# Attention into a snake MLP on one core: both token halves of two head pairs finished as one in the first stage

## The chip, the cores and the metric

The kernel runs on one core of a Trainium2 chip. The metric is the device time of one execution in microseconds (us). The kernel before took 214.25, 214.41 and 214.91 us in three runs, a median of 214.41 us. One execution was also recorded by the hardware profiler; every duration below comes from that record.

## The reference

Attention over chunks of 32 tokens, each chunk seeing 8 memory rows, itself, 16 tokens to the left and 8 to the right; then, per token, a feed-forward layer with the activation h + sin²(αh)/α.

```python
B, H, S, D = 4, 8, 768, 64              # batches, heads, tokens, head width
for c in range(S // 32):                # scores are scaled by 1/sqrt(D)
    k_full = concat([mem_k, k[:, :, l_start:r_end]])
    v_full = concat([mem_v, v[:, :, l_start:r_end]])
    a = softmax(scale * q_c @ k_full.T)
    out[:, :, chunk] = a @ v_full
x = out.transpose(0, 2, 1, 3).reshape(B * S, H * D)      # 3072 x 512
h = x @ w_in                                             # 512 x 2048
g = h + sin(alpha * h) ** 2 / alpha
return g @ w_out                                         # 2048 x 512
```

## The kernel before

**Tiling.** Tokens are taken in windows of 96 (three chunks), eight windows to a batch; a *half* is four windows, 384 tokens. Heads go in pairs (`hp`, 0 to 3). A window's keys lie in 128 columns of the transposed keys `kT`: 64 context keys, 8 memory keys, 56 more. Scores are computed keys by tokens, so that `exp` gives the tile `pt` (128 keys x 768: two heads of a pair by four windows of 96) which is at once the stationary operand of the product with the values `vw`. A 65th column of `vw` holds ones, so that each value product also gives the sum of the exponentials; `normed` (L352) takes the reciprocal of that column (L355, on VectorE) and multiplies (L356, VectorE, 96 x 512) into a block `x_blk`. Four transposes on TensorE (L368) and one copy (L371, 128 x 384) turn such a block into `xT`, the input of the feed-forward layer with the channels on the partitions.

**Stages.** Batch 0's attention is done alone, in a first stage; then four stages follow, each doing the feed-forward layer of one batch while the attention of the next is woven into it. In a stage the layer's first product (L426) makes tiles of 128 hidden channels by 768 tokens, a `sin` (L441, ScalarE), a square (L449 or L446) and L453 (VectorE) finish each, and the second product (L464) is fed in between. The first stage is the only one that this change touches.

**Order.** The order is written out by hand, as words that are carried out from left to right; each word issues its instructions to the engines, and every engine runs its own in that order, waiting for semaphores where data or buffers are not ready. The words that matter here, with `hp` and half as digits:

- `k2`, `l2`: transposes of the keys and queries of pair 2 (L276, 12 on TensorE); `K2V`, `L2V`: their copies to `kT` and `qT` (L287 or L301, last letter A for ScalarE, V for VectorE; after each `K` a small VectorE copy L293 of the ends)
- `a6V`: the cast of the third pair's queries to bf16 on VectorE (L655)
- `s01`: scores of pair 0, half 1 (`u_scores`: two mask products L319, eight score products L327, then `exp` L334 on ScalarE)
- `v01`: their value products and normalisation (`u_values`: eight products L346, then L355 and L356)
- `T01`, `t10`: transposes and copy into `xT`, on ScalarE (`T`) or VectorE (`t`)
- `z1`: a product of zeros (L688), 512 columns; it keeps TensorE at work
- `dm`, `I02`, `I27`: loads of the memory values and of `w_in` on GpSimd's queue (L667, L213); `Cs`: two fills of `kst` on GpSimd (L810, L811); `Ws`: loads the table for `sin` on ScalarE (L701)
- `V068`: the values of pairs 3 (heads 6 and 7) on GpSimd's queue (L172, L179)

PSUM has eight banks. `Banks` (L59) hands out a bank or an even pair of banks, the longest free first; scores, value products and a feed-forward tile take a pair, transposes one. `Slots` (L45) hands out six `x_blk` buffers in the same way. The kernel ends the first stage with `Ws`; the next stage begins with `b0 h0`, the first tile of L426 (four products for half 0, which need the half 0 of all four pairs in `xT`, then four for half 1).

## Time and profile before

| what | us |
|---|---|
| median of three runs | 214.41 (214.25 to 214.91) |
| the profiled execution, its own time | 215.01 |
| its span, first to last instruction | 213.2 |
| first L426 product starts (end of the first stage on TensorE) | 24.91 |
| TensorE clock granted | 1.0 throughout |

| group in the first stage, 12 to 25 us | count | mean us of one |
|---|---|---|
| L334 `exp`, ScalarE | 8 | 0.822 |
| L356 multiply 96 x 512, VectorE | 8 | 0.687 |
| L355 reciprocal 96 x 8, VectorE | 8 | 0.196 |
| L346 value products, 65 columns, TensorE | 64 | 0.195 |
| L371 copies into `xT`, ScalarE, 128 x 384 | 4 | 0.478 |
| L371 copies into `xT`, VectorE, 128 x 384 | 4 | 0.344 |
| L301 copies of 128 x 768, ScalarE | 2 | 0.830 |
| L701 load of the `sin` table, ScalarE | 1 | 1.283 |

How to read it: products on TensorE are pipelined, so that a group's length is set by the spacing of its starts and not by the sum of the durations. "Idle before" in a line is the time in which the engine did nothing ahead of the instruction, with what released it; "issue" there means that the engine waited for nothing that the profile shows.

### The profile page before, as it was taken

The page shows a single profiled execution, that of the slowest core. Times are in us where ns is not written, and L with a number is a line of the kernel's source. Part 1 is how long each engine was busy: PE and PEld are TensorE (multiplying, and loading weights), DVE is VectorE, ACT ScalarE, POOL GpSimd, SP SyncE. Part 2 cuts the span into 40 slices and gives each one's busy share as a digit, 9 for nine tenths or more (in the row PEclk, how much of TensorE's full clock was granted, in tenths as well). Part 3 has the DMA queues.
Part 4 walks back from the last instruction along what each step waited for, and adds up shares of the span by engine and source line. Part 5 has one row for each costly group of instructions (what it writes and reads, how often), then busy time and mean ns, then how long its engine had stood idle before and what let it go on. Part 6 is the DMA issues. An engine that isn't in the chain of part 4 may idle for free.

```text
span 213.2 us, 4484 instructions
## 1 busy us (share of the span) xinstructions
PE 203.4 (95%) x1716; PEld 114.9 (54%) x1736; DVE 140.0 (66%) x218; ACT 143.3 (67%) x229; POOL 99.9 (47%) x142
## 2 busy tenths in 40 slices
PE   7888899999999999999999999999999999999994
PEld 2366665565555556555455555554555565654453
DVE  4788788999542749975856649897257187865010
ACT  2588898976857469978846199887846189891110
POOL 8989505589596197109993038664000022200000
PEclk9999999999999999999999999999999999999999
DMA  5999999999999999999993259999944400000312
GB/s 153 311 169 141 209 207 204 205 149 184 126 170 155 163 122 137 146 112 171 144 215 95 71 124 126 170 128 126 134 101 108 135 3 0 2 3 0 148 49 98
DMA packets 95852, 27.80 MB, mean 130 GB/s; under 512 B 84808, under 2 KB 92376, under 8 KB 95832
## 3 DMA queue, kind: packets, MB, share of 16 engines
q0 software_dynamic: 69152, 13.64, 84.7%
q1 hardware_dynamic: 25720, 12.68, 28.3%
q10 hardware_dynamic: 960, 1.21, 1.7%
q8 instruction: 13, 0.21, 0.5%
q14 instruction: 7, 0.06, 0.1%
HBM read 29.66 MB, written 6.29 MB: 169 GB/s over the span
## 4 chain that ended last, share of the span: by engine, by line
PE 74%; DVE 9%; ACT 5%; DMA 5%; issue 4%; POOL 1%; DVEq 0%; ACTq 0%
PE ps L464 37%; PE ps L426 29%; DMA kq_f<-in_k_dram 4%; DVE gT L453 3%; PE ps L416 3%; DVE s L449 3%; PE ps L387 2%; ACT pt L334 2%; ACT u L441 2%; ACT s L446 2%; PE ps L368 1%; POOL s L449 1%; DMA memk_f<-in_mem_k_dram 1%; DVE kT L287 1%; DVE x_blk L356 1%
## 5 line engine op out<-in xcount | busy, mean ns | idle before, releaser
L464 PE MATMUL ps<-w_out_sb,gT 128*128 128x512 bf16 (+1 forms) x382 | 86.9, 370 | 1.3 <-issue 0.3
L426 PE MATMUL ps<-xT,w_in_sb 128*128 128x384 bf16 x512 | 85.9, 326 | 0.6 <-DVE gT L453 0.4
L453 DVE SCALAR_TENSOR_TENSOR gT<-s,inv_alpha,ps 128x768 bf16<-128x768 f32 x64 | 63.1, 1012 | 12.3 <-ACT s L446 5.2
L426 PEld LDWEIGHTS <-w_in_sb 128*128 128x128 bf16 x512 | 49.8, 98 | 35.1 <-issue 1.7
L441 ACT ACTIVATE u<-ps,alpha_sb 128x768 f32<-128x768 f32 x64 | 56.6, 894 | 16.9 <-PE ps L426 14.4
L464 PEld LDWEIGHTS <-gT 128*128 128x128 bf16 x400 | 37.1, 98 | 37.2 <-DVE gT L453 0.2
L449 POOL TENSOR_TENSOR s<-u 128x768 f32<-128x768 f32 x11 | 17.2, 1567 | 69.1 <-ACT u L441 57.0
L401 ACT ACTIVATE pt<-ps,biasm 128x256 bf16<-128x256 f32 x72 | 27.2, 488 | 10.5 <-PE ps L387 10.5
L471 DVE COPY o_sb<-ps 128x512 f32<-128x512 f32 (+1 forms) x15 | 10.0, 669 | 27.4 <-PE ps L464 25.5
L449 DVE TENSOR_TENSOR s<-u 128x768 f32<-128x768 f32 x23 | 21.9, 953 | 7.6 <-ACT u L441 7.5
L446 ACT ACTIVATE s<-u 128x768 f32<-128x768 f32 x30 | 25.0, 841 | 0.5
L356 DVE TENSOR_TENSOR x_blk<-ps,rinv 96x512 bf16<-96x512 f32 x32 | 22.0, 687 | 1.1
L471 ACT COPY o_sb<-ps 128x512 f32<-128x512 f32 (+1 forms) x10 | 5.7, 572 | 21.7 <-PE ps L464 21.7
L172 POOL DMA_DIRECT2D vw<-in_v_dram x13 | 12.2, 939 | 6.7 <-PE ps L368 6.2
L355 DVE RECIPROCAL rinv<-ps 96x8 f32<-96x8 f32 x32 | 6.4, 199 | 13.2 <-PE ps L416 12.7
L179 POOL DMA_DIRECT2D vw<-in_v_dram x13 | 13.3, 1024 | 1.7 <-DMA vw<-in_v_dram 1.3
L232 POOL DMA_DIRECT2D kst<-in_k_dram x16 | 11.1, 691 | 2.7 <-DMA vw<-in_v_dram 2.1
L238 POOL DMA_DIRECT2D kst<-in_k_dram x16 | 12.1, 758 | 0.2 <-issue 0.2
L245 POOL DMA_DIRECT2D q_bf<-in_q_dram x12 | 10.7, 910 | 0.0
L371 ACT COPY xT<-ps 128x384 bf16<-128x384 bf16 x10 | 4.9, 496 | 8.4 <-PE ps L368 8.2
L416 PEld LDWEIGHTS <-pt 128*128 128x128 bf16 x192 | 8.2, 97 | 4.2 <-ACT pt L401 0.3
L688 PE MATMUL ps<-zeros 128*128 128x512 bf16 x24 | 8.3, 488 | 1.2 <-DVE tiny L725 1.2
(82 smaller groups left out, 137.2 us busy)
## 6 DMA issues: line engine op xcount, KB each, us to landing
out_dram<-o_sb SPq DMA_DIRECT2D x23, 256.0 KB, 2.2
q_bf<-in_q_dram POOLq DMA_DIRECT2D x12, 128.0 KB, 6.6
kq_f<-in_k_dram SPq DMA_DIRECT2D x3, 384.0 KB, 6.6
kq_f<-in_q_dram ACTq DMA_DIRECT2D x3, 384.0 KB, 8.8
w_in_sb<-in_moe_w_in_dram POOLq DMA_DIRECT2D x1, 1152.0 KB, 12.6
vw<-in_v_dram POOLq DMA_DIRECT2D x7, 128.0 KB, 7.9
vw<-in_v_dram POOLq DMA_DIRECT2D x8, 112.0 KB, 8.0
kst<-in_k_dram POOLq DMA_DIRECT2D x14, 64.0 KB, 4.9
```

The source lines that it names most:

```text
L172: nc.gpsimd.dma_start(vw[0:64, lo:c1, 0:D], win(vflat, a, n, 64))
L179: nc.gpsimd.dma_start(vw[72:128, c0:hi, 0:D], win(vflat, base + QW * c0 + 48, hi - c0, 56))
L356: nc.vector.tensor_tensor(out=x_blk[:].rearrange("p g e d -> p e g d"), in0=otv[0:QW, :, :, 0:D], in1=rinv[:].unsqueeze(3).to_broadcast([Q ...
L401: nc.scalar.activation(pt[:, 0:H * QW].rearrange("p (g e c) -> p g e c", g=2, e=4)[:, :, :, 32 * m:32 * m + 32], sc[:, :, 0:4 * QW].rearra ...
L416: nc.tensor.matmul(otv[:, e, hp, :], pt[:, QW * i:QW * i + P], vws[b % 2][:, 2 * hp + e, j, 0:D + 1],)
L426: nc.tensor.matmul(t["hT"][:, hf, 0:HALF], w_in_sb[:, kt, P * t["ft"]:P * t["ft"] + P], t["xT"][:, kt, HALF * hf:HALF * hf + HALF], start= ...
L441: nc.scalar.activation(t["u"][:], t["hT"][:, :, 0:HALF], ACTF.Sin, scale=alpha_sb[:, ft:ft + 1])
L446: nc.scalar.activation(s2[:], u[:], ACTF.Square)
L449: e.tensor_tensor(out=s2[:], in0=u[:], in1=u[:], op=ALU.mult)
L453: nc.vector.scalar_tensor_tensor(out=gT[:, ft, :].rearrange("p (e c) -> p e c", e=2), in0=t["s2"][:], scalar=inv_alpha[:, ft:ft + 1], in1= ...
L464: nc.tensor.matmul(o[:, c0:c1], gT[:, ft, P * s:P * s + P], w_out_sb[:, ft, c0:c1], start=(ft == 0), stop=(ft == FT - 1),)
L471: copier(state["engines"][state["o"] % len(state["engines"])])(o_sb[:, c0:c1], o[:, c0:c1])
```

## The change

For pairs 0 and 1 of batch 0 both halves are finished together. A new word `n12` (pair 1, "2" for both halves) makes the sums by products with a column of ones, 16 for a pair, and one reciprocal of 96 x 16. `v12` then makes the 16 value products without the 65th column and one multiply of 96 x 1024 into a buffer of two blocks, and `T12` does eight transposes and one copy of 128 x 768 into `xT`. Pairs 2 and 3 go on as before. The six `x_blk` buffers become three tiles of two. The words of the first stage after `V046` are reordered; what comes before stays.

```diff
+    def take_two(self, pairs):
+        at = {id(t): n for n, t in self.free}
+        two = min((p for p in pairs if id(p[0]) in at and id(p[1]) in at),
+                  key=lambda p: max(at[id(p[0])], at[id(p[1])]))
...
+    ones = consts.tile([P, 1], BF, name="ones")
...
-    xslots = Slots([consts.tile([QW, HP, 2, D], BF, name=f"x_blk{i}") for i in range(6)])
+    x_two = [consts.tile([QW, 2, HP, 2, D], BF, name=f"x_two{i}") for i in range(3)]
+    xpairs = [(t[:, 0], t[:, 1], t) for t in x_two]
+    xslots = Slots([h for t in xpairs for h in t[0:2]])
...
+    def u_sums(b, hp, units):
+        bank, bs = banks.single()
+        n = len(units)
+        for e in range(2):
+            for u, pt in enumerate(units):
+                for i in range(4):
+                    c = (e * n + u) * 4 + i
+                    nc.tensor.matmul(
+                        bank[:, c:c + 1], pt[:, HALF * e + QW * i:HALF * e + QW * i + P], ones[:],
+                    )
+        rinv = blk.tile([QW, 2, 4 * n], F32, name="rinv_u", bufs=4)
+        nc.vector.reciprocal(rinv[:], bank[0:QW, 0:8 * n].rearrange("p (e g) -> p e g", e=2))
...
+    def u_mixed(b, hp, half, units, rinv):
+        ot, bs = banks.pair()
+        n = len(units)
+        otv = ot[:, :, 0:4 * n * D].rearrange("p e (g c) -> p e g c", c=D)
+        for u, pt in enumerate(units):
+            for e in range(2):
+                for i in range(4):
+                    nc.tensor.matmul(
+                        otv[:, e, 4 * u + i, :], pt[:, HALF * e + QW * i:HALF * e + QW * i + P],
+                        vws[b % 2][:, 2 * hp + e, 4 * (half + u) + i, 0:D],
+                    )
...
+        nc.vector.tensor_tensor(
+            out=out, in0=otv[0:QW], in1=rinv[:].unsqueeze(3).to_broadcast([QW, 2, 4 * n, D]), op=ALU.mult,
+        )
...
+    def u_turn_two(xT, hp, x_blk, eng):
+        bank, bs = banks.single()
+        xtp = bank[:, 0:S // 2].bitcast(BF).rearrange("p (g c) -> p g c", c=QW)
+        for g in range(8):
+            nc.tensor.transpose(
+                xtp[:, g, :], x_blk[2][:, g // 4, g % 4].rearrange("p e d -> p (e d)"), ident[0:QW, 0:QW]
+            )
+        copier(eng)(xT[:, hp, :].rearrange("p (g c) -> p g c", c=QW), xtp)
...
+    nc.vector.memset(ones[:], 1.0)
...
-        'K0A a6V L1A s00 s10 s11 K2V l2 k3 L2V K3A s01 v11 dm l3 L3A v10 s20 v01 s30 v00 s31 v30 s21 '
-        'v31 z1 T01 v20 T30 I02 Cs T00 v21 t10 T20 t31 z1 t11 I27 t21 Ws '
+        'K0A K2VA a6V L1A s00 s11 s10 s01 l2 L2V k3 n12 K3AV v12 l3 n02 L3A v02 s30 s31 s20 v30 v31 '
+        's21 T12 v20 dm z1 I02 T30 v21 T02 I27 t20 T31 z1 z1 Ws Cs t21 '
```

In `K2VA` and `K3AV` only the first letter after the digit is read; the second does nothing in this kernel.

More of the change, by code (lines that the diff above doesn't have):

```diff
@@ L53, in take @@
         return self.free.pop(min(range(len(self.free)), key=lambda i: self.free[i][0]))[1]
+    def take_two(self, pairs):
+        at = {id(t): n for n, t in self.free}
+        two = min((p for p in pairs if id(p[0]) in at and id(p[1]) in at),
+                  key=lambda p: max(at[id(p[0])], at[id(p[1])]))
+        self.free = [f for f in self.free if f[1] is not two[0] and f[1] is not two[1]]
+        return two
     def give(self, t, late=0):
@@ L339, in u_scores @@
         return pt
+    def u_sums(b, hp, units):
[10 more added lines that the diff above has]
+        nc.vector.reciprocal(rinv[:], bank[0:QW, 0:8 * n].rearrange("p (e g) -> p e g", e=2))
+        banks.give(bs)
+        return rinv
+    def u_mixed(b, hp, half, units, rinv):
[9 more added lines that the diff above has]
+                    )
+        if n == 2:
+            x_blk = xslots.take_two(xpairs)
+            out = x_blk[2][:].rearrange("p u g e d -> p e (u g) d")
+        else:
+            x_blk = xslots.take()
+            out = x_blk[:].rearrange("p g e d -> p e g d")
+        nc.vector.tensor_tensor(
+            out=out, in0=otv[0:QW], in1=rinv[:].unsqueeze(3).to_broadcast([QW, 2, 4 * n, D]), op=ALU.mult,
+        )
+        banks.give(bs)
+        return x_blk
+    def u_turn_two(xT, hp, x_blk, eng):
[6 more added lines that the diff above has]
+        copier(eng)(xT[:, hp, :].rearrange("p (g c) -> p g c", c=QW), xtp)
+        banks.give(bs)
     def u_values(b, hp, half, pt):
@@ L512, in __init__ @@
             self.done = 0
+            self.rinv = {}
             self.nx = None
@@ L603, in do_s, with do_n @@
                 self.pt.update(scores(self.b, [int(c) for c in a]))
+        def do_n(self, a):
+            hp, half = int(a[0]), int(a[1])
+            units = [self.pt[a]] if half < 2 else [self.pt[a[0] + "0"], self.pt[a[0] + "1"]]
+            self.rinv[a] = u_sums(0, hp, units)
         def do_v(self, a):
-            if self.b == 0:
+            if self.b == 0 and a in self.rinv:
+                hp, half = int(a[0]), int(a[1])
+                units = [self.pt.pop(u) for u in ([a] if half < 2 else [a[0] + "0", a[0] + "1"])]
+                self.xb[a] = u_mixed(0, hp, half % 2, units, self.rinv.pop(a))
+            elif self.b == 0:
                 self.xb[a] = u_values(0, int(a[0]), int(a[1]), self.pt.pop(a))
@@ L613, in turn_x @@
             x_blk = self.xb.pop(a)
+            if self.b == 0 and a[1] == "2":
+                u_turn_two(x, int(a[0]), x_blk, eng)
+                for half in x_blk[0:2]:
+                    xslots.give(half)
+                return
             if self.b == 0:
```

## The prediction

> **What bounds the kernel now.** I read the page's shares first, then TensorE's waits, then the first stage engine by engine, because only that stage's code differs.

> ```profile
> span 213.2 us, 4484 instructions
> PE 203.4 (95%) x1716; PEld 114.9 (54%) x1736; DVE 140.0 (66%) x218; ACT 143.3 (67%) x229; POOL 99.9 (47%) x142
> ...
> PE   7888899999999999999999999999999999999994
> ...
> q8 instruction: 13, 0.21, 0.5%
> ```

> TensorE (PE) is full from the sixth slice (about 25 us) on. The waits of TensorE from 25 us to the end, one row each (us in all, times, longest):

> ```profile
> PE ps L426 <- DVE gT L453: 0.4, 2, 0.2
> PE ps L464 <- issue: 0.3, 2, 0.2
> PE ps L464 <- ACT qT L301: 0.2, 1, 0.2
> PE ps L387 <- DVE kT L293: 0.2, 1, 0.2
> ```

> They sum to 1.1 us, and none waits for a load. So after the first stage nothing can absorb a delay or waste a gain: the time moves by as much as the first L426 product moves, which is at 24.91 us now. In the first stage the chain of waits and the timeline of TensorE and of ScalarE show one hole:

> ```profile
> 19.20 0.34 PE L319 MATMUL ps<-mind,mrow 64*128 64x384 bf16 x2
> 19.38 0.20 PE L327 MATMUL ps<-qT,kT 64*128 64x96 bf16 x1
> 20.23 0.33 PE L327 MATMUL ps<-qT,kT 64*128 64x96 bf16 x7 [0.64 <-issue]
> ...
> 20.59 1.61 ACT L334 ACTIVATE pt<-ps 128x768 bf16<-128x768 f32 x2 [0.82 <-PE ps L327]
> ```

> The scores of pair 3, half 1 (`s31`) stop after one of eight products, with "issue" as the releaser, and ScalarE's `exp` chain stands 0.82 us behind it. Nothing that these products read is late. Three rows explain it. (a) The page has 13 transfers of kind "instruction" on queue q8, 0.21 MB, so 16 KB each; only TensorE's program (3501 instructions in the kernel's order, ScalarE's 239, VectorE's 223) is long enough for them. (b) 3501 less 449, over 12 or 13 transfers, is 254 or 235 instructions each, and the product that runs at 20.23 is TensorE's 450th instruction (the rows count 220 products and 222 weight loads up to 20.00 us). (c) The first q8 transfer falls at 17.0 to 17.1 us, the second at 24.3 to 24.5, while the DMA engines are full. I read the hole as TensorE's code arriving late: instruction 450 exists for it only from 20.2 us.

> **The change, part by part.** *What it does to the hole.* Up to the first score product the TensorE order is the same (183 instructions), so that the code is asked for at the same time, and the loads queued ahead of it are the same: I keep 20.2 us. In the changed order TensorE's 450th instruction is the weight load for the second half in `v02`. To see when it gets there, from rows (`exp` starts 0.70 apart when fed: 14.00, then three in 2.22; a value or transposed pair 0.03 to 0.04; a score group about 0.5, 0.35 when the next follows):

> - four `exp` run from 14.00 to 16.9 (three do now, to 16.2); `K3A` on ScalarE follows to 17.6.
> - VectorE now does `K2V` (0.84 and 0.26) before the cast `a6V` (1.28), which ends at 15.3 instead of 14.22; `l2` starts at 15.3 (now 14.87), `k3` ends at 16.25. Cover: `n12` needs the third `exp`, until 16.23 anyway. Without that cover it would cost 0.4.
> - `n12` (16.3), `v12` (to 17.4), `l3` (17.2 to 17.8), `n02` (17.6), `v02` from 18.0; its ninth weight load at 18.3.

> TensorE then stands from 18.3 to 20.2: 1.9 us in place of 0.64. Queued behind it are the rest of `v02`, and all four of `s30 s31 s20 s21`; in the kernel now only the rest of `s31` and `s21` are. ScalarE ends `L3A` at 18.6 and waits.

> *What is left from 20.2 us.* The rest of `v02` 0.25; `s30` to 21.02; `exp` of `s30`, `s31`, `s20` at 21.06, 21.76, 22.45 (the last ends 23.26). `s21` is queued behind `v30 v31`, and `v31` needs the second `exp` (22.56): value products to 23.0, `s21` to 23.41, its `exp` 23.45 to 24.26. Then ScalarE's copies in order: `T12` 24.15 to 24.98 (0.83, the row of L301, same shape), `T30` to 25.34, `T02` to 26.12, `T31` to 26.5. The first L426 needs `T02`: 26.17 against 24.91, **+1.26**. The `sin` table (1.283 and 0.20) follows `T31`: the first L441 at 27.9 against 26.41, +1.5, but the second, paced by TensorE, at 29.05 against 27.76, +1.29. The fifth tile's L426 waits for the first L453, which ends at 29.43 now and at 30.9 then; TensorE gets there at 26.17 + 5.25 = 31.4. So +1.26 stays.

> *The single costs in it.* VectorE loses four reciprocals and four multiplies (4 x 0.196 + 4 x 0.687 = 3.53) and gains two of each; the multiply of 1024 is not in the trace: 0.69 to 1.37 (one or two of the old), I take 1.2, since L449 and L453, 768 long, take 0.95 to 1.01; the reciprocal of 16 is 0.20 to 0.39, L793's 0.25 the nearest. That is 2.9: 0.6 saved where VectorE waits for TensorE. A multiply of 1.4 would move L426 by 0.1. One-column products: 32, between 0 and 0.033 each (L346: eight starts in 0.23), at most 1.1 in all, before 20.2, where TensorE would stand anyway; were there no hole, they are in the schedule below at 0.025 (four L774 in 0.25, of which one's own length is 0.17). ScalarE's copies grow from 4 x 0.43 to 2 x 0.8 + 2 x 0.45, +0.8, on the path; VectorE's shrink from four to two. `ones`: 0.06 on VectorE at 1.2 us, under its wait for `ident` until 1.35. One more `z1`, 0.22, while TensorE waits for `T02`. GpSimd's queue: `dm` and `I02` keep their order, `I27` passes `Cs` and is issued 1.06 earlier (17.24 for 18.30), landing 7.8 us later at 25 for 26; the third tile needs it at 27.5 now, 28.8 then: nothing gained. `Cs` fills are wanted by stage one's row loads, after 49 us. SP's queue is untouched. The three two-block buffers only change which block is used; the later multiplies wait for the same things.

> [...]

> *Sum.* 213.2 + 1.26 = 214.46 in span, 216.3 for such an execution with the 1.8 around it; the median of the runs stands 0.6 under the profiled execution, so 214.41 + 1.26 = **215.67**.

> **The rivals.**

> *The hole is a load, not code (not slower).* The values of pair 3 (L179, issued at 12.25, some 8 us to land) arrive at about 20.2 as well, and `v30` behind `s31` waits for them. For it: the coincidence. Against: the seven products held are scores, which read no values, and stand ahead of the wait. If so, the changed kernel has no hole, since it wants those values later: `v02` ends at 18.6, `exp` of `s30` starts at 19.1, of `s21` at 21.5, `T02` ends at 24.54, first L426 at 24.6, that is -0.3: **214.1**. From the same schedule: it decides if TensorE's code is there by 18.5 us, for whichever cause; between 18.5 and 20.2 each us earlier takes one off. Code at 19.5 would give 24.5 before and 25.45 after, +0.95.

> *A second hole.* The next boundary is 235 to 254 instructions on; at 254 it falls some 27 instructions into the feed-forward (28.4 us; now at 31.8). Its code was moved at 24.4, and at the first boundary 20.2 - 17.1 = 3.1 us passed between move and use: 27.5. For: 0.9 of margin where there were 4.4. Against: the DMA engines carry larger packets by then. A hole to 29 to 30 would add some 0.7: **216.4**. [...]

> *The end is set elsewhere.* Were the loads of `w_in` the limit, the shift would vanish. The 1152 KB one lands 12.6 us after 19.05, at 31.7, and tile 7 wants it at 34; nothing speaks for it.

> **How the numbers follow.** Forecast 0.68, second hole 0.08, no hole 0.20, the rest 0.04. A measurement of this kernel tells about 0.3% (0.64 us) from no change: the runs before spread by that much. The forecast and the second hole are slower, 0.76. No hole at -0.3 is within, 0.12 of its 0.20; with copies or multiplies cheaper than assumed it passes -0.64, 0.08. The rest (code at 18.9 to 19.2) is within: 0.16 in all. The likeliest's own range is 215.0 to 216.2 (code 0.7 earlier or 0.5 later); to hold eight in ten with the rivals: 214.0 to 216.4.

> **What would show it.** TensorE idle "issue" before the ninth weight load of `v02`, up to about 20.2, 1.5 to 2 us long; ScalarE's fifth `exp` at about 21.0; first L426 at 26.2; the rest of the timeline shifted rigidly. Wrong if the wait is missing or elsewhere, or if the first L426 starts under 25.3 us.

## The result, and the profile after

The changed kernel took 216.27 us (median of 21 runs, 214.86 to 218.18), the kernel before beside it 214.60 (21 runs, 214.15 to 215.87). The ratio is 1.0063 (95% interval 1.0043 to 1.0083): slower by 1.35 us (the two medians lie 1.67 apart), where +1.26 and 215.67 in all were forecast, between 214.0 and 216.4. One run of the changed kernel, at 218.18 us, over 1.5% above the fastest, is left out of the ratio and of the means below.

The page of the changed kernel, shares and slices (the columns are those of the page before):

```profile
span 214.4 us, 4572 instructions
PE 206.8 (96%) x1769; PEld 116.2 (54%) x1769; DVE 138.6 (65%) x213; ACT 143.6 (67%) x229; POOL 99.9 (47%) x142
...
PE   7897999999999999999999999999999999999994
...
PEclk9997899999999999999999999999999999999999
...
q8 instruction: 14, 0.23, 0.5%
```

Two things are new: the fourth and fifth slices of TensorE's granted clock, and one more transfer of code (14 for 13). The timeline of TensorE in the first stage, changed kernel:

```profile
17.27 0.55 PE L358 MATMUL ps<-ones,pt 128*128 128x1 bf16 x16
17.68 0.40 PE L373 MATMUL ps<-vw,pt 128*128 128x64 bf16 x8
19.19 0.55 PE L373 MATMUL ps<-vw,pt 128*128 128x64 bf16 x8 [1.10 <-issue]
19.67 0.50 PE L329 MATMUL ps<-mind,mrow 64*128 64x384 bf16 x2
19.97 0.53 PE L337 MATMUL ps<-qT,kT 64*128 64x96 bf16 x8
20.29 0.52 PE L329 MATMUL ps<-mind,mrow 64*128 64x384 bf16 x2
...
26.04 1.14 PE L484 MATMUL ps<-xT,w_in_sb 128*128 128x384 bf16 x6
```

`v02` stops after eight of its sixteen products, for "issue", and goes on at 19.19: the place that the prediction named, the 450th instruction. L484 is L426 of the kernel before; its first product comes at 26.04 instead of 24.91. ScalarE's timeline has the same stop behind it:

```profile
17.38 0.80 ACT L311 COPY qT<-ps 128x768 bf16<-128x768 bf16 x1 [0.29 <-PE ps L286]
20.54 2.21 ACT L344 ACTIVATE pt<-ps 128x768 bf16<-128x768 f32 x3 [2.36 <-PE ps L337]
23.25 0.81 ACT L344 ACTIVATE pt<-ps 128x768 bf16<-128x768 f32 x1 [0.50 <-PE ps L337]
23.95 0.79 ACT L396 COPY xT<-ps 128x768 bf16<-128x768 bf16 x1
24.63 0.50 ACT L429 COPY xT<-ps 128x384 bf16<-128x384 bf16 x1
25.14 0.80 ACT L396 COPY xT<-ps 128x768 bf16<-128x768 bf16 x1
```

TensorE's waits from 25 us to the end are as few as before, and from the first L484 product to the end the two profiles take 188.37 and 188.33 us: the shift of 1.13 is the shift of the end.

```profile
PE ps L484 <- DVE gT L511: 0.4, 2, 0.2
PE ps L445 <- DVE kT L303: 0.2, 1, 0.2
```

What the prediction did not have is the clock. Busy time by stretch, changed kernel (start, end and length of the stretch; busy us and, in brackets, instructions of TensorE, its weight loads, VectorE, ScalarE and GpSimd; then the granted clock, DMA share and GB/s):

```profile
15.90:19.29 3.39, 2.29 (x72) 2.02 (x72) 2.13 (x5) 1.98 (x3) 3.34 (x6) 1.00 3.38 138
19.30:22.70 3.40, 3.40 (x54) 2.55 (x54) 1.52 (x3) 2.16 (x3) 3.39 (x5) 0.50 1.42 196
22.72:26.10 3.38, 3.33 (x63) 2.47 (x63) 3.24 (x8) 2.87 (x6) 1.11 (x3) 1.00 1.15 214
```

From 19.30 us, just behind the stop, TensorE runs at half its clock for 3.41 us. In the timeline above the mask products of `s30` and `s31` start 0.62 apart (19.67, 20.29), where a score group took 0.35 when fed.

### The profile page after: what moved, and what is told of

Its sections match the earlier page's. It is cut to its first block, busy times and chain, and to the rows that moved or that the text cites. A ratio compares the mean times of both kernels' runs of the same rounds, so it can differ in the third digit from the quotient of the medians.

```text
span 214.4 us, 4572 instructions
## 1 busy us (share of the span) xinstructions
PE 206.8 (96%) x1769; PEld 116.2 (54%) x1769; DVE 138.6 (65%) x213; ACT 143.6 (67%) x229; POOL 99.9 (47%) x142
## 3 DMA queue, kind: packets, MB, share of 16 engines
q10 hardware_dynamic: 960, 1.21, 1.7%
## 4 chain that ended last, share of the span: by engine, by line
PE 80%; DVE 9%; ACT 5%; issue 4%; POOL 1%; DVEq 0%
PE ps L522 37%; PE ps L484 28%; DVE gT L511 3%; PE ps L761 3%; PE ps L474 3%; DVE s L507 3%; PE ps L445 2%; ACT u L499 2%; ACT s L504 2%; PE ps L426 1%; PE ps L286 1%; POOL s L507 1%; DVE kT L297 1%; ACT pt L344 1%; PE ps L329 1%
## 5 line engine op out<-in xcount | busy, mean ns | idle before, releaser
L522 PE MATMUL ps<-w_out_sb,gT 128*128 128x512 bf16 (+1 forms) x400 | 89.1, 371 | 0.0
L484 PE MATMUL ps<-xT,w_in_sb 128*128 128x384 bf16 x512 | 85.9, 326 | 0.6 <-DVE gT L511 0.4
L484 PEld LDWEIGHTS <-w_in_sb 128*128 128x128 bf16 x512 | 49.7, 98 | 35.3 <-issue 2.0
L507 POOL TENSOR_TENSOR s<-u 128x768 f32<-128x768 f32 x11 | 17.2, 1567 | 70.5 <-ACT u L499 58.4
L414 DVE TENSOR_TENSOR x_two<-ps,rinv 96x512 bf16<-96x512 f32 x28 | 19.2, 687 | 1.0
L413 DVE RECIPROCAL rinv<-ps 96x8 f32<-96x8 f32 x28 | 5.6, 199 | 13.9 <-PE ps L474 11.3
L189 POOL DMA_DIRECT2D vw<-in_v_dram x13 | 13.3, 1024 | 1.8 <-DMA vw<-in_v_dram 1.5
L248 POOL DMA_DIRECT2D kst<-in_k_dram x16 | 12.4, 774 | 1.1 <-DMA vw<-in_v_dram 0.9
L242 POOL DMA_DIRECT2D kst<-in_k_dram x16 | 11.3, 708 | 1.4 <-DMA vw<-in_v_dram 1.4
L761 PE MATMUL ps<-zeros 128*128 128x512 bf16 x27 | 9.2, 473 | 1.2 <-DVE tiny L798 1.2
L429 ACT COPY xT<-ps 128x384 bf16<-128x384 bf16 x8 | 4.0, 504 | 7.7 <-PE ps L426 7.7
```

The lines of the kernel that those rows point to most:

```text
L189: nc.gpsimd.dma_start(vw[72:128, c0:hi, 0:D], win(vflat, base + QW * c0 + 48, hi - c0, 56))
L414: nc.vector.tensor_tensor(out=x_blk[:].rearrange("p g e d -> p e g d"), in0=otv[0:QW, :, :, 0:D], in1=rinv[:].unsqueeze(3).to_broadcast([Q ...
L484: nc.tensor.matmul(t["hT"][:, hf, 0:HALF], w_in_sb[:, kt, P * t["ft"]:P * t["ft"] + P], t["xT"][:, kt, HALF * hf:HALF * hf + HALF], start= ...
L507: e.tensor_tensor(out=s2[:], in0=u[:], in1=u[:], op=ALU.mult)
L522: nc.tensor.matmul(o[:, c0:c1], gT[:, ft, P * s:P * s + P], w_out_sb[:, ft, c0:c1], start=(ft == 0), stop=(ft == FT - 1),)
L761: nc.tensor.matmul(ps[:, b, :], zeros[:, 0:P], zeros[:])
```

## The experiments

Theory 1 is the prediction's: TensorE's code from instruction 450 on is late; what the change does is to add 64 weight loads and products (the one-column sums) ahead of that place, and to queue four scores behind it. Theory 2: the hole waits for a load of values. Theory 3: the merged work itself costs the time.

**More instructions, same work.** `a_cut24` (changed kernel) and `b_cut24` (kernel before) cut the first 24 products of zeros in two, 48 TensorE instructions more.

```diff
-        'z1 z1 z1 Ci z1 a4A We z1 Cb a1A z1 z2 z1 z1 dq068 ...
+        'y1 y1 y1 Ci y1 a4A We y1 Cb a1A y1 y2 y1 y1 dq068 ...
+        def do_y(self, a):
+            b = min(banks.given, key=banks.given.get)
+            for _ in range(int(a)):
+                for c in (0, 256):
+                    nc.tensor.matmul(ps[:, b, c:c + 256], zeros[:, 0:P], zeros[:, c:c + 256])
```

> The changed kernel with 24 of the early one-instruction zero products (512 columns) cut into two of 256: same work, 24 products and 24 weight loads more on TensorE ahead of the 450th instruction, all of them before the first score. Theory 1 (the hole is TensorE's code from instruction 450 on arriving late, some 6.2 to 6.9 us after its 194th instruction): the hole moves back in content by 48 instructions, to the second-half products of n02 or the last of v12 (reached at about 17.1 us), is asked for some 0.7 us earlier (the 194th instruction is then in the transposes of k2) and ends at 18.5 to 19.2, so 1.4 to 2.1 us long; exps five to eight as in the changed kernel or 0.3 later; time 0 to +0.6 us against the changed kernel, +1.2 to +2.3 against the kernel before. Theory 2 (the hole is the wait for a load): the hole stays before the ninth weight load of v02 at 19.2, n02 runs at 17.2 without a stop. Theory 3 (the merge's own work costs the time): as the changed kernel, no matter where the hole is.

> The kernel before with the same 24 zero products cut in two: nothing of the change in it, 48 TensorE instructions more ahead of the first score. Theory 1: TensorE's 450th instruction is then the second product of v01, reached at 17.5 to 18.1 us; a hole of 1 to 1.7 us stands there, ending at about 19.2, and the hole inside s31 is gone; the first L426 product starts 0.1 to 0.4 later than in the kernel before; if a hole of over 1 us also halves the granted clock for 3.4 us, as the changed kernel's trace shows, +0.9 more, so +0.1 to +1.3 us in all. Theory 2: the hole stays inside s31, 0.64 us, at 19.6 to 20.2, and the time is that of before. Theory 3: no difference from before.

`a_cut24`: 215.71 us, 1.0026 (0.9998 to 1.0053). The first hole is gone, not moved: the code's packet started at 14.37 instead of 16.34, and `n02` ran at 17.37 without a stop. A second one stands at the 706th instruction, 256 after the 450th (the prediction has the next boundary 235 to 254 on); TensorE's timeline has it inside the transposes of pair 2 (`t20`):

```profile
23.38 0.22 PE L426 MATMUL ps<-ident,x_two 96*128 96x96 bf16 x1
24.31 0.46 PE L426 MATMUL ps<-ident,x_two 96*128 96x96 bf16 x7 [0.71 <-issue]
...
25.21 0.98 PE L484 MATMUL ps<-xT,w_in_sb 128*128 128x384 bf16 x5
```

`b_cut24`: 214.46 us, 0.9979 (0.9951 to 1.0006). No hole inside `s31` and none at the new place; the first L426 product at 24.34, 0.57 before that of the kernel before. What TensorE waits for now is a load of values:

```profile
20.73 0.34 PE L368 MATMUL ps<-ident,x_blk 96*128 96x96 bf16 x4
21.73 0.41 PE L346 MATMUL ps<-vw,pt 128*128 128x65 bf16 x8 [0.67 <-DMA vw<-in_v_dram]
```

So the hole goes with the place of an instruction and not with the work that stands there; the fixed delay of 6.2 to 6.9 us that I had given the code does not hold.

**The order without the merge.** `a_order` keeps the changed order of scores, but finishes pairs 0 and 1 half by half.

```diff
-        's00 s11 s10 s01 l2 L2V k3 n12 K3AV v12 l3 n02 L3A v02 s30 s31 s20 v30 v31 '
-        's21 T12 v20 dm z1 I02 T30 v21 T02 I27 t20 T31 z1 z1 Ws Cs t21 '
+        's00 s11 s10 s01 l2 L2V k3 v10 K3A v11 l3 L3A v00 v01 s30 s31 s20 v30 v31 s21 '
+        'T10 v20 dm z1 I02 T30 t11 v21 T00 I27 t01 T20 t31 z1 z1 Ws Cs t21 '
```

> The changed kernel's order of loads, scores and casts, but pairs 0 and 1 finished half by half with ones columns as before: no sum products, no merged multiply, no merged copies (ScalarE and VectorE copy two each). The 450th TensorE instruction falls into the score products of s31 or s20, reached at about 19.7. Theory 1: no hole of over 0.3 us (the code is there by 19.2 to 20.2), the clock stays at 1.0; the first L426 product is +0.55 us later than before by the order alone (four scores stand behind v00 and v01), so +0.3 to +0.8 us, and 0.7 to 1.5 under the changed kernel. Theory 2: the same, as the loads are the same. Theory 3 (the merge itself costs the time): the time of before, within 0.3 us. If the order were the whole cost, the time of the changed kernel, +1.35.

215.62 us, 1.0029 (1.0006 to 1.0051). No wait for code over 0.1 us and no fall of the clock in any of its 12 runs, as theory 1 has it; the first L484 at 25.89, 0.98 later than before. In this profile the order alone costs more than the 0.55 expected: TensorE waited 1.3 us for VectorE's multiplies and 0.6 us for values.

**The instructions without the change.** `b_ones` is the kernel before with 32 unused one-column products.

```diff
-        '... s01 v11 dm l3 L3A v10 s20 ...
+        '... s01 n11 v11 dm l3 L3A n10 v10 s20 ...
+        def do_n(self, a):
+            bank, bs = banks.single()
+            for c in range(16):
+                nc.tensor.matmul(bank[:, c:c + 1], self.pt[a][:, 0:P], ones[:])
+            banks.give(bs)
```

> The kernel before with 32 unused one-column products (16 ahead of v11, 16 ahead of v10; their results are dropped): 64 TensorE instructions more, about 0.8 us of TensorE's own work ahead of s20. Theory 1: the 450th instruction is a weight load of s30, reached at about 18.6; a hole of 0.6 to 1.6 us stands there up to 19.2 to 20.2, all of s30, s31 and s21 behind it; first L426 +0.7 to +1.4 us (and up to 0.9 more if the hole is over 1 us and the clock falls). Theory 2: hole where it was, ahead of v30, and only the 32 products' own time: 0 to +0.35 us. Theory 3: 0 to +0.35 us.

215.97 us, 1.0055 (1.0021 to 1.0090), nearly the changed kernel's loss with nothing merged and no order changed. TensorE's timeline:

```profile
18.06 0.29 PE L328 MATMUL ps<-qT,kT 64*128 64x96 bf16 x6
19.33 0.22 PE L328 MATMUL ps<-qT,kT 64*128 64x96 bf16 x2 [0.98 <-issue]
```

The scores of `s30` stop after six of eight products, exactly before the 450th instruction. They read no values, and the load that theory 2 names had landed at 18.99 (in the changed kernel at 18.48, 0.7 us before its stop ended). The clock was halved from 19.79 to 23.20. Theory 2 falls here.

**A smaller dose, split copies, an idle TensorE.** Three kernels with only 8 products of zeros cut: as such (`a_cut8`), with the merged blocks copied out in two halves (`a8_split`), and with a wait for ScalarE put between `v02` and `s30` (`a8_idle`).

```diff
-        copier(eng)(xT[:, hp, :].rearrange("p (g c) -> p g c", c=QW), xtp)
+        for h in range(2):
+            copier(eng)(
+                xT[:, hp, HALF * h:HALF * h + HALF].rearrange("p (g c) -> p g c", c=QW), xtp[:, 4 * h:4 * h + 4],
+            )
...
-        '... L3A v02 s30 ...
+        '... L3A v02 j6 s30 ...
+        def do_j(self, a):
+            for _ in range(int(a)):
+                nc.scalar.copy(junk[:], zeros[:, 0:256])
+            b = min(banks.given, key=banks.given.get)
+            nc.tensor.matmul(ps[:, b, :], junk[:, 0:P], zeros[:])
```

> The changed kernel with 8 of the early zero products cut in two (16 TensorE instructions more, ahead of everything in dispute): the 194th instruction falls into the transposes of k2 (12.4 us) instead of the first score (13.05), the 450th is the first weight load of v02, the 706th lies in the second group of feed-forward products behind the first L484. Theory 1 (code late): the code comes at 18.2 to 18.6, a hole of 0.3 to 0.9 us before v02, under the length that halved the clock; no second hole, which cost the kernel with 24 cuts 0.8 us at 23.4 to 24.3; first L484 at 24.4 to 24.9 where the changed kernel has 26.04, time 214.3 to 215.2, that is 1.0 to 1.9 under the changed kernel and level with the one before. Theory 3 (merge or order cost the time): first L484 at 25.2 or later, time 215.6 as with 24 cuts, whatever the hole is.

> As the one with 8 cuts, but each merged transposed block is copied out in two copies of 384 columns in place of one of 768 (T12 and T02 on ScalarE), so that half 0 is out before half 1. [...] If the first L484 is paced by the transposes behind (t20, T31 and two zero products stand ahead of it on TensorE) rather than by T02: 0 to 0.1 us, which cannot be told from none.

> As the one with 8 cuts, but between v02 and s30 ScalarE makes six copies of 256 columns into a spare tile and one TensorE product reads it, so that TensorE stands for 1.2 to 2.0 us for ScalarE, with its code there. If any idle of TensorE of over about 1 us halves the granted clock: clock 0.5 for some 3.4 us from the end of that wait on, s30 s31 s20 0.64 apart. If the fall of the clock belongs to the fetch of code: clock 1.0 throughout and score groups 0.35 apart.

`a_cut8`: 216.81 us, 1.0097 (1.0062 to 1.0132). The place came out as forecast, the time did not: TensorE stood at the first product of `v02`, again the 450th instruction, from 18.2 to 19.82, though its 194th instruction now lies ahead of the first score. The load that these products read had landed at 17.20. (The view names VectorE's reciprocal, which was done at 19.12.)

```profile
17.73 0.55 PE L358 MATMUL ps<-ones,pt 128*128 128x1 bf16 x16
19.82 1.03 PE L373 MATMUL ps<-vw,pt 128*128 128x64 bf16 x16 [1.54 <-DVE rinv_u L362]
```

Seven of its eight runs had a granted clock of 0.982 to 0.992. `a8_split`: 216.75 us, 1.0102 (1.0050 to 1.0155); the split copies bring nothing that can be told. Its profile, by stretch, gives something else:

```profile
17.88:21.27 3.39, 1.76 (x46) 1.37 (x46) 2.04 (x3) 1.14 (x3) 2.87 (x5) 1.00 2.41 162
21.29:24.69 3.40, 3.04 (x65) 2.47 (x66) 2.70 (x7) 3.14 (x6) 2.85 (x4) 1.00 1.18 210
```

TensorE stood 1.47 us at the same place and kept its clock; its first feed-forward product came 6.31 us after the stop's end, in `a_cut8` 7.17. The difference, 0.86 us, I put down to the halved clock; it is one profile against one. `a8_idle`, 218.02 us (two runs, 1.0136, 1.0068 to 1.0205), tells nothing of its question: the code came only at 19.91, after 2.07 us of standing, and the wait for ScalarE behind it was short; its clock was halved from 20.32 to 23.74.

**What the code waits for.** The packets of queue q8 have their times in the trace. One packet of 16 KB, the first of them in the kernel, brings, as I read it, the code from instruction 450 on; it takes 1.3 to 1.6 us. In us, from eight of the profiles (the last column: when the granted clock was 0.5):

```
kernel     194th instr.   packet starts (later by)   450th runs   stop before it   clock halved
before        13.38          17.06  (3.7)               20.23        0.64           no
changed       13.05          16.34  (3.3)               19.18        1.10           19.30-22.71
b_ones        13.04          16.12  (3.1)               19.32        0.98           19.79-23.20
a_cut8        12.94          16.66  (3.7)               19.82        1.54           19.53-22.94
a8_split      12.52          16.36  (3.8)               19.33        1.47           no
a_cut24       11.93          14.37  (2.4)               17.37        none           no
b_cut24       11.93          14.02  (2.1)               17.83        none           no
a_nov         14.38          15.44  (1.1)               19.36        none           no
```

Where TensorE stood, it went on 1.4 to 1.8 us after the packet's end. That the code is asked for at the 194th instruction, 256 ahead, is an estimate of mine, from the 256 instructions between the stops at the 450th and the 706th and from the next packets of the changed kernel, which start 3.6 and 1.7 us after its 450th and 706th. The packet's start varies by more than its length: something keeps it. `a_nov` and `b_nov` leave out a load that is in the queues when the 194th instruction runs.

```diff
             b, h0, h1 = (int(c) for c in a)
+            if (b, h0) == (0, 6):
+                for _ in range(2):
+                    nc.gpsimd.memset(vws[0][:, h0:h1, :, 0:D], 0.0)
+                return
             load_v(b, h0, h1)
```

> The changed kernel without the load of the values of head pair 3 (two 112 to 120 KB loads, issued at 11.0 and 12.0 us); two GpSimd memsets of the same tile stand in their place, so pair 3's values are zeros. Instructions of TensorE unchanged. Queue theory (the code's packet waits behind the loads already in the DMA queues): its packet starts 1 us or more earlier than 16.34, the code is there by 18.2, the hole before the ninth weight load of v02 is under 0.4 us or gone, the clock stays at 1.0, and first L484 comes at 24.4 to 24.9: the merge without a hole, 214.3 to 215.2. Fixed-delay theory (the code comes 6.1 to 6.9 us after the 194th instruction, whatever is in the queues): hole until 19.1 or later, first L484 at 25.2 to 26.1, time 215.3 to 216.5. Merge theory (the merged work costs the time): 1.2 us over the next kernel, whatever the hole is.

> The kernel before with the same load replaced by the same memsets: the base for the last one. Queue theory: the code is there before TensorE gets to instruction 450 inside s31 (19.6), no hole, first L426 at 24.4 to 24.6, 0.3 to 0.5 us under the kernel before, and the changed one within 0.3 us of it. Fixed-delay theory: hole to 20.0, time of before. If the hole in the kernel before was the load of these values (theory 2), it goes as well, but then b_ones's hole ahead of s30 has no cause.

The packet started 1.06 and 0.87 us after the 194th instruction, against 2.1 to 4.4 in all the profiles with the load. That is what code that queues behind loads would do; in these two the 194th instruction also came later, at 14.38 and 14.08, so that a queue emptier for that reason is not ruled out. `a_nov` has no hole before the 450th instruction, and its view of TensorE's waits in the first stage (us in all, times, longest) is led by the merged multiply:

```profile
PE ps L404 <- DVE x_two L383: 0.7, 1, 0.7
PE ps L426 <- DVE x_two L414: 0.2, 1, 0.2
```

The times are less clean: the memsets put the whole first stage off by a us, and in `b_nov` the clock fell at 14.15 (in half of the runs of both it was lowered). `a_nov` took 216.53 us (1.0064, 1.0040 to 1.0088), `b_nov` 215.83 (1.0040, 1.0022 to 1.0059): 0.7 us between them, neither the 0.3 of the queue theory nor the 1.2 of theory 3. By the runs whose granted clock stayed at 0.998 and more it is 0.3 us (216.13 in 4 runs, 215.81 in 6). The first feed-forward product came at 25.72 and 25.56, where 24.4 to 24.9 and 24.4 to 24.6 were expected. So with the code there, merge and new order together cost some 0.3 to 0.7 us; these two kernels don't tell the one from the other.

In `b_nov` the clock fell without any wait for code: in the 3.41 us before, TensorE stood 1.15 and 0.77 us for VectorE's casts.

**Two kernels once more.** `b_cut24r` is `b_cut24` again, `after2` the changed kernel again.

> The kernel before with 24 zero products cut in two once more, for more rounds: the first time its ratio was 0.9979 (0.9951 to 1.0006) and its first L426 product 0.57 us ahead of the one before. If that is the hole that is gone and no clock drop: 0.997 to 0.999 again, no run with a granted clock under 0.995. If it was chance: 1.000.

> The changed kernel once more, for a second profile and for the spread of its runs. Code theory: a stop at the same instruction (the ninth weight load of v02) for the third thing that differs, its end, at 18.5 to 20.2, and the first L484 product 6.0 to 6.3 us after that end if the clock stays, 6.8 to 7.2 if it is halved. Clock grid theory (the granted clock is reconsidered every 3.413 us on a grid that does not start with the kernel, so that the same stop sometimes costs the clock and sometimes not): a third to a half of the runs at a granted clock of 0.984 to 0.992, these 1.0 to 1.6 us longer than the rest; a fall, if the profile has one, on the grid counted from the first rise of the clock. If the fall belongs to the change itself, all runs at 0.992 or less.

`b_cut24r`: 215.12 us, 1.0008 (0.9983 to 1.0032). In this profile a load of values landed at 19.44 (17.36 the first time), and `v01` stood for it:

```profile
19.57 0.55 PE L346 MATMUL ps<-vw,pt 128*128 128x65 bf16 x8 [1.24 <-DMA vw<-in_v_dram]
```

Over both, cutting the products gains nothing that can be told, and no kernel tried here beats the one before. `after2`: 217.21 us (6 runs), 1.0108 (1.0076 to 1.0139). TensorE's timeline and the stretches:

```profile
17.40 0.40 PE L373 MATMUL ps<-vw,pt 128*128 128x64 bf16 x8
19.89 0.42 PE L373 MATMUL ps<-vw,pt 128*128 128x64 bf16 x8 [2.10 <-issue]
```

```profile
18.03:21.42 3.39, 1.52 (x38) 1.13 (x38) 1.42 (x3) 0.63 (x1) 2.51 (x4) 1.00 2.20 165
21.44:28.25 6.81, 6.50 (x76) 5.13 (x77) 3.93 (x10) 5.03 (x9) 3.40 (x5) 0.50 1.15 213
```

The same place, the stop twice as long (2.10 us for 1.10), and the clock halved for 6.83 us; the first L484 at 28.32, 8.43 after the stop's end for 6.86. Five of the six runs had a granted clock of 0.982 to 0.992, where a third to a half was expected.

## Why the prediction was right, point by point

- *The end moves by as much as the first L426 product.* Right: 24.91 to 26.04, and 188.33 and 188.37 us from there to the end.
- *The hole is code that is late.* Right as to what stops: in six kernels TensorE stands before its 450th instruction, in scores (`b_ones`, the kernel before), in the middle of `v02` (the changed kernel, twice) or at its start (`a_cut8` and the two made from it), and the next boundary is the 706th (`a_cut24`), 256 further on.
- *The code comes at 20.2 in both kernels.* This is the term of the sum that was mis-sized: 19.18 in the profile compared, 19.89 in the second. I kept the time because the instructions and loads ahead are the same. They are, but the code's packet starts anywhere from 2.1 to 4.4 us after the 194th instruction, and the loads in the queues are the likely cause. The stop was 1.10 us and not 1.9 (2.10 in the second profile).
- *From the code's arrival 5.97 us to the first L426.* It took 6.86; the 0.89 more is about what the halved clock cost `a_cut8` against `a8_split` (0.86), and no step of mine had the clock, here halved for 3.41 us. `a8_split`, with the clock kept, took 6.31 from 8 products further back, which is some 0.3 of work: about 6.0, so that the schedule's length held.
- The two errors nearly cancel in that profile: 1.0 us less of stop, 0.9 more of clock. That the number came out is in good part luck. Over the runs the mean is 216.24 (20 runs), 1.4 above the 214.82 of the kernel before. The 12 runs at a granted clock of 0.998 and more have a mean of 215.65, +0.8; the 8 at 0.992 and less 217.12, +2.3. That such runs also have the longer stops is likely and not shown, so the clock's part of the mean is 0.6 at most. How the rest divides is not settled: the new order without merge, stop or fall of the clock is already +0.6 (`a_order`), the kernel before with 32 unused products, a stop and at times the halved clock +1.2 (`b_ones`). The two are no parts of one sum.
- *Single costs.* The multiply of 96 x 1024 took 1.21 (1.2 taken), the reciprocal of 96 x 16 0.25 (0.25), sixteen one-column products 0.55 with the last one's own length of 0.16, 0.026 each (0.025), the copies of 768 0.80 (0.83). `a6V` was over-estimated: it took 0.55, not 1.28, and ended at 14.41.
- *Split copies.* They save nothing that can be told: 1.0102 split, 1.0097 not. TensorE is not there earlier: twelve transposes and two products of zeros stand ahead of the first L484, the last of them at 25.85 in the changed kernel, where `T02`'s copy ends at 25.94. So the last wait of my sum, the first L426 for `T02`, was not what held it: TensorE came to it only at 26.04, by its own order.
- *The rivals.* A load (theory 2) is refuted by `b_ones`; the second hole did not come in the changed kernel, whose 706th instruction ran at 27.83 without a stop, but `a_cut24` had it there, 0.71 us long. The third, an end set elsewhere, falls with the first point. For early code I had given the changed kernel -0.3 us; `a_nov` against `b_nov` says some 0.3 to 0.7 more, so that this part of the schedule was too favourable: TensorE waits 0.7 us there for the merged multiply. And the order costs where it isn't merged: `a_order` has neither hole nor fall of the clock and is 1.0029.

## What to carry to other kernels

On a chain that TensorE's own program sets, instructions can be a cost of their own: 32 unused products, 64 instructions, cost 1.2 us in `b_ones`, its stop and the clock included. TensorE stood here before its 450th and its 706th instruction: count to such places, see whether the code can be there when the engine arrives, and ask what a few dozen more instructions ahead of it will push behind it. The code came here by DMA as the loads do, in packets of 16 KB; its packet started 2.1 to 4.4 us after the 194th instruction with the values of pair 3 in the queues, and 0.87 and 1.06 us without, so a stage that fills the DMA queues may delay its own program. After a stop the clock can be halved, for 3.41 and 6.83 us in the two profiles of the changed kernel and not at all in that of `a8_split`, and one profile shows only one draw of that: judge it by the granted clock of all runs (lowered in 14 of the changed kernel's 27).

## What the runs showed of the hardware

How long the stop is doesn't decide alone: 1.47 us (`a8_split`) left the clock. Nor does TensorE's busy time: 2.29 us of the 3.41 before the changed kernel's fall, 1.76 of the 3.41 that held `a8_split`'s stop. By the runs' granted clocks it fell in 14 of 27 runs of the changed kernel, 4 of 12 of `b_ones`, 7 of 8 of `a_cut8`, 4 of 6 of `a8_split`, 1 of 12 of `a_cut24`, 3 of 84 of the kernel before in the later comparisons, 0 of 24 of `b_cut24` and its repeat and 0 of 12 of `a_order`.

One count does separate the steps. Weigh each product by its columns, times its size in the timeline as a share of 128*128: a score product (64*128, 96 columns) counts 48, a product with `ones` 1, a feed-forward product 384; a step of 21 feed-forward products holds 8064. In the 13 profiles the six steps before these falls hold 1488 to 2816, all other steps up to 190 us that ran at full clock 2960 or more, `a8_split`'s with the stop 3328. By this the changed kernel's 32 products with `ones`, which keep TensorE busy for 1.1 us, count next to nothing for the clock. It was counted after the fact, the margin is narrow, no run varied it alone, and what makes the clock rise again is not covered. So what within a step decides stays open.
